# Loop loads moved behind the last weight turns, two more gradient buffers, and row halves in the head of a fused forward and backward block

## The chip, the cores and the metric

The kernel runs on one core of one Trainium2 chip. The time is the device time of one execution in microseconds (us); lower is better. A profile is one execution recorded instruction by instruction, and its span runs from the first to the last instruction.

## The reference

The reference returns the output of a block and all its gradients, for 2048 rows of width D = 576 and a hidden width F = 4608:

```python
mod = (_silu(c) @ w_mod).reshape(c.shape[0], 6, 1, -1)      # sa, ca, ga, sb, cb, gb
h = _layernorm(x) * (1 + ca) + sa
x = x + ga * irfft2(rfft2(h) * (w_r + 1j * w_i))
h = _layernorm(x) * (1 + cb) + sb
x = x + gb * einsum('bsf,fd->bsd', (h @ w_gate) * (h @ w_up), w_down)
...
_out, _vjp = jax.vjp(_f, A_x, A_w_r, A_w_i, B_w_gate, B_w_up, B_w_down, c, w_mod)
_grads = _vjp(grad_out)
```

What matters here is one product of the backward pass: the gradient of the hidden layer, `ghh = (grad_out * gb) @ w_down^T`, of shape 2048 x 4608. Everything in the loop over the hidden width needs it.

## The kernel before

Rows are kept 128 to a tile, 16 tiles; the hidden width is cut in 36 blocks of 128 columns. The kernel has a head, a loop over the 36 blocks, and a tail.

**The head** does three things. It runs the forward spectral layer in three stages: stage 1 (`s1_*`) norms and transforms the rows, stage 2 (`s2_*`) filters, stage 3 (`s3_*`) transforms back, norms again and makes `h2p` (the second normed input); every fourth step of stage 3 turns four tiles of it into `h2T` with a transposing DMA on SP's queue (four such turns in all). Into these stages, and after them, it deals the `u4` work, which computes `ghh` block by block and stores it in `ghhT_d` in DRAM. The chip is kept busy with `u4` matmuls where the spectral stages wait; about half of `u4` is left when stage 3 ends, and is run to its end alone.

**The u4 work.** `goT` holds `grad_out * gb` turned by TensorE (PE) in stage 1 (16 tiles, five 128-column pieces each; width 576 is four and a half pieces, so the fifth piece is half padding). For two blocks at a time, `w_down` is loaded into `wdn` (two buffers) and turned by a transposing DMA into `wdT` (five buffers); these DMAs are in the list `turns`, 18 of them. One block is four groups; a group is five matmuls of 128x512 into one PSUM bank, one per piece, and a copy by ScalarE (ACT) or VectorE (DVE), in turn, from the bank into `ghh_st`. After four groups GpSimd (POOL) issues the store of `ghh_st`, 512 KB, to `ghhT_d`. `ghh_st` has two buffers, so the copies of a block wait until the store of the block two before it has landed. `u4` has three PSUM banks; the spectral stages have the other five (`fps`).

**The loop.** For each block it needs `wgu` (columns of `w_gate` and `w_up`, loaded for two blocks at a time, gate on SP's queue, up on POOL's), `ghh` (from `ghhT_d`, on POOL's queue), and for each four blocks `wT`, ten transposing DMAs of `w_gate` and `w_up` on SP's queue. The matmuls of `h2T` with `wgu` come first (`gup`); in them the half piece of width 64 is already done with row halves: gate's 64 rows sit on partitions 0 to 63 and up's on 64 to 127, so that two matmuls use one half of TensorE's rows each ("corners", L606). The `u8` matmuls, which need `wT`, start with the second block.

**What sets the order.** Each engine runs its instructions in one fixed order, which a scheduler in the compiler makes from priorities, buffers and dependences. `tc.issue_after(i)` adds the condition that what follows stands behind `i` on `i`'s engine. In the kernel before, the loop's first loads have no such condition, and the first `wT` is tied to the seventh- to third-last turns: the loads of `wgu` and `ghh` for the first blocks come to stand in the queues in the middle of the `u4` work, between the last two `h2T` turns.

Of the kernel before, what the change touches and what calls it, by code (L numbers as in the profile page):

```python
# [19 lines left out]
NT = 16  # L20
S = 2048
D = 576
DP = 640
# [59 lines left out]
def build(ctx, tc, A_x, A_w_r, A_w_i, B_w_gate, B_w_up, B_w_down, c_in, w_mod, grad_out,  # L83
          out_0, out_1, out_2, out_3, out_4, out_5, out_6, out_7, out_8):
    nc = tc.nc
# [11 lines left out]
    def dram(name, shape, dt):  # L97
        return nc.dram_tensor(name, list(shape), dt).ap()
# [3 lines left out]
    modb_d = dram("modb_d", [128, 6, D], BF)  # L102
# [4 lines left out]
    ghhT_d = dram("ghhT_d", [F, S], BF)  # L107
# [4 lines left out]
    MSA, MCA, MGA, MSB, MCB, MGB = range(6)  # L112
# [8 lines left out]
    ident = glob.tile([128, 128], BF, name="ident")  # L121
# [12 lines left out]
    def evac(dst, src, eng=None):  # L134
        if eng is None:
            eng = "a" if cnt[0] % 2 == 0 else "v"
            cnt[0] += 1
        if eng == "a":
            nc.scalar.copy(dst, src)  # L139
        else:  # L140
            nc.vector.tensor_copy(dst, src)  # L141
# [42 lines left out]
    gonf = res2.tile([128, NT * D + 64], BF, name="gon")  # L184
    gon = gonf[:, 0:NT * D].rearrange("p (t d) -> p t d", t=NT)

    with ExitStack() as hs:
        def pool(name, bufs, side="left", space=None, stack=hs):
            kw = dict(name=name, bufs=bufs, reuse_waits="tile")
            if space is not None:  # L190
                kw["space"] = space
            else:
                kw["side"] = side
            return stack.enter_context(tc.tile_pool(**kw))

# [46 lines left out]
        def mod_make(j, wm, eng="v"):  # L242
            for h in range(2):
                ps = fps.tile([128, 512], FP32, name="modps", tag="fp")
                for m in range(5):
                    nc.tensor.matmul(ps[:, 0:288], lhsT=sc_rep[:, m, :], rhs=wm[:, m, h * 288:(h + 1) * 288], start=(m == 0), stop=(m == 4))
                if j in (MCA, MCB):
                    nc.vector.tensor_scalar(out=modh[j][:, h * 288:(h + 1) * 288], in0=ps[:, 0:288], scalar1=1.0, scalar2=None, op0=ADD)
                else:
                    evac(modh[j][:, h * 288:(h + 1) * 288], ps[:, 0:288], eng=eng)  # L250
            return nc.sync.dma_start(modb_d[:, j, :], modh[j][:]).ins
# [28 lines left out]
        Vv = VA[:].rearrange("k (g t c f) -> k g t c f", g=NG, t=NT, c=2)  # L280
        hTs, zts, n1s = {}, {}, {}
        gbT = hp1.tile([128, 5], BF, name="gbT")
        nc.gpsimd.memset(gbT[:], 0.0)

        def s1_norm(t):
            c4, tt = t // 4, t % 4
# [24 lines left out]
        def s1_cols(t):  # L311
            zt = zts[t] = hw2.tile([128, 2, FP], BF, name="zt", bufs=3)
            for cc in range(2):
                zp = fps.tile([128, 512], FP32, name="zp", tag="fp")
                for m in range(5):
                    mm = nc.tensor.matmul(zp[:, :FP], lhsT=hTs[t][:, m, :], rhs=T["RD"][:, m, cc, :], start=(m == 0), stop=(m == 4))  # L316
                evac(zt[:, cc, :], zp[:, :FP], eng="a")
            if t == 1:
                with tc.issue_after(mm.ins):
                    mod_make(MGB, wms[MGB], "a")  # L320
                with nc.allow_non_contiguous_dma(reason="tiny column load"):
                    nc.sync.dma_start(gbT[:, 0:4], modb_d[0, MGB, 0:512].rearrange("(m q) -> q m", q=128))
                    nc.sync.dma_start(gbT[0:64, 4:5], modb_d[0, MGB, 512:576].rearrange("(m q) -> q m", q=64))

        def s1_rows(t):
            zt = zts[t]
# [14 lines left out]
        nc.gpsimd.dma_start(wn_d, wn[:].rearrange("k c a f -> k (c a f)"))  # L341
        goT = u4.tile([128, NT, 5, 128], BF, name="goT")
        for t in range(NT):
            pt = u4ps.tile([128, 5, 128], BF, name="u4p")
            for m in range(5):
                nc.tensor.transpose(pt[:, m, :], gonf[:, t * D + m * 128:t * D + (m + 1) * 128], ident[:])
            nc.vector.tensor_tensor(out=goT[:, t, :, :], in0=pt[:], in1=gbT[:].unsqueeze(2).to_broadcast([128, 5, 128]), op=MUL)
        FB4 = 2
        turns, wdTs, sts, u4_done, u4r = [], {}, {}, [0], []

        def u4_group(g, eng=None):
            fb, sb4 = g // 4, g % 4
            k, j = fb // FB4, fb % FB4
            if g % (4 * FB4) == 0:
                wdTs[k] = (u4w if not u4r or k % 5 < 2 else u4r[0]).tile([128, FB4, 5, 128], BF, name="wdT")
                wdn = wdn2[:, k % 2, :, :]
                with tc.issue_after(first):
                    nc.sync.dma_start(wdn[:, :, 0:D], B_w_down[fb * 128:(fb + FB4) * 128, :].rearrange("(j f) d -> f j d", f=128))
                turns.append(nc.sync.dma_start_transpose(out=wdTs[k][:].rearrange("q j m f -> q (j m) f"), in_=wdn.rearrange("f j d -> f (j d)")).ins)
            if sb4 == 0:  # L360
                sts[fb] = u4w.tile([128, NT, 128], BF, name="ghh_st", bufs=2)
            pt = u4ps.tile([128, 4, 128], FP32, name="u4p")
            for m in range(5):
                nc.tensor.matmul(pt[:], lhsT=wdTs[k][:, j, m, :], rhs=goT[:, 4 * sb4:4 * sb4 + 4, m, :], start=(m == 0), stop=(m == 4))  # L364
            evac(sts[fb][:, 4 * sb4:4 * sb4 + 4, :], pt[:], eng=eng)
            if sb4 == 3:
                nc.gpsimd.dma_start(ghhT_d[fb * 128:(fb + 1) * 128, :], sts[fb][:].rearrange("f t p -> f (t p)"))

        def u4_groups(n, eng=None):
            for _ in range(n):  # L370
# [70 lines left out]
            T["IR"] = load_table(hp1, "IR", "tA")  # L441
        r2.close()
        u4r.append(pool("u4r", 3, "right"))
        hw2 = pool("hc3", 2, "right")


# [60 lines left out]
    with ExitStack() as ms:  # L507
# [13 lines left out]
        with ExitStack() as bs:  # L521
            FBW = 2
# [112 lines left out]
            def u8_output(fbs, t, h):  # L635
# [8 lines left out]
                else:  # L644
                    nc.vector.tensor_tensor(out=dst, in0=dst, in1=pu[:, 0:288], op=ADD)  # L645

            for fb in range(NFB):
                if fb % FBW == 0:
                    wgu = wp.tile([128, 9, FBW * 128], BF, name="wgu")
                    for wi_, wsrc in enumerate((B_w_gate, B_w_up)):  # L650
                        eng = nc.sync if wi_ == 0 else nc.gpsimd
                        eng.dma_start(wgu[:, 4 * wi_:4 * wi_ + 4, :], wsrc[0:512, fb * 128:(fb + FBW) * 128].rearrange("(m q) f -> q m f", q=128))
                        eng.dma_start(wgu[64 * wi_:64 * wi_ + 64, 8, :], wsrc[512:576, fb * 128:(fb + FBW) * 128])
                if fb == 0:
                    wTs[0] = wT_load(0, turns[-7:-2])
                ghh = ghp.tile([128, NT, 128], BF, name="ghh")
                nc.gpsimd.dma_start(ghh[:].rearrange("f t p -> f (t p)"), ghhT_d[fb * 128:(fb + 1) * 128, :])
                trip[fb] = [p.tile([128, NT, 128], BF, name=nm) for p, nm in ((tp2, "gT"), (tp2, "uT"), (tp, "hhT"), (tp, "ggT"), (tp, "guT"))] + [ghh, wgu]
                main = gup_items(fb, 0)
                if fb >= 2:  # L660
                    main += product(fb - 2, 2)
                main += gup_items(fb, 1)
                turn_at = len(main)
                main.append(turn_items(fb))
                if 1 <= fb < NFB - 1:
                    main += product(fb - 1, 0) + product(fb - 1, 1)
                outs = [(fb - 1, t, h) for t in range(NT) for h in range(2)] if 1 <= fb < NFB - 1 else []
                dealt = 0
                for k, f in enumerate(main):
# [17 lines left out]
    with ExitStack() as ts:  # L687
# [383 lines left out]
        for tp_ in range(NT // 2):  # L1071
# [13 lines left out]
            for ti in range(2):  # L1085
                t = 2 * tp_ + ti
# [16 lines left out]
                stored = nc.gpsimd.dma_start(o0_v[:, t, :], o0[:])  # L1103
# [87 lines left out]
```

## Time and profile before

| | |
|---|---|
| median of 3 runs | 1605.65 us (1599.14 to 1614.77) |
| the profiled execution | 1611.72 us, of which the span is 1609.9 us |
| mean granted TensorE clock | 0.989 |
| PE busy | 1542.1 us (96%) |
| stretch with least PE work in the head | 200 to 250 us: PE busy 33.59 of 50 us, clock 0.83 |
| first matmul of the loop | 298.05 us |

Busy time of PE is modelled from pipelined matmuls; a stretch in which PE shows less than its full length is one in which it had nothing to run. The granted clock is the share of full speed that the throttle allowed. A DMA's "time to landing" is from its issue to its last semaphore update.

### The profile page before, as it was taken

What the parts mean: (1) busy time and instruction counts of PE and PEld (TensorE: products, weight loads), DVE (VectorE), ACT (ScalarE), POOL (GpSimd) and SP (SyncE); (2) the same over time, 40 slices, a digit from 0 to 9 for tenths busy, and PEclk for the clock granted to TensorE, in tenths of its full rate; (3) what the DMA queues carried; (4) which work ended last, traced back from release to release, by engine and by line L of the source; (5) the groups of instructions that cost most, each with busy time, mean ns of one, the idle gap of its engine ahead of it and who ended that gap; (6) DMA issues with size and microseconds to landing.
All of it is one profiled execution on the core that took longest, in us unless ns stands there. A gap on an engine that the chain in (4) does not pass through costs nothing.

```text
span 1609.9 us, 29989 instructions
## 1 busy us (share of the span) xinstructions
PE 1542.1 (96%) x11354; PEld 1041.0 (65%) x11354; DVE 1038.4 (65%) x2610; ACT 559.1 (35%) x1108; POOL 170.4 (11%) x284
## 2 busy tenths in 40 slices
PE   6999959999999999999999999999999979899997
PEld 4666624466766666666766666666667666677775
DVE  6765743566666666666666666666666765678656
ACT  6666712322222222222222222222222365466022
POOL 0001311100101010000101010100100011100232
PEclk9999979999999999999999999999999999999998
DMA  9978998488778677685767877776866786636775
GB/s 320 278 213 230 266 191 193 134 149 158 146 149 145 139 145 151 129 165 116 159 149 136 159 138 146 137 164 114 169 123 132 193 256 195 227 114 180 281 216 162
DMA packets 482995, 280.36 MB, mean 174 GB/s; under 512 B 405377, under 2 KB 450178, under 8 KB 481954
## 3 DMA queue, kind: packets, MB, share of 16 engines
q1 hardware_dynamic: 457666, 185.38, 55.4%
q0 software_dynamic: 25184, 93.07, 19.6%
q8 instruction: 88, 1.44, 0.4%
q14 instruction: 57, 0.47, 0.1%
HBM read 108.51 MB, written 82.31 MB: 119 GB/s over the span
## 4 chain that ended last, share of the span: by engine, by line
PE 77%; DMA 11%; DVE 5%; ACT 3%; issue 3%; POOL 0%; SPq 0%; DVEq 0%; ACTq 0%; POOLq 0%
PE u57p L558 25%; PE u8p L640 17%; PE gup L611 15%; PE u4p L364 7%; DMA ghhT_d<-ghh_st 2%; PE gup L606 2%; PE u3p L1091 2%; DMA Xn<-xn_d 2%; DMA n2c<-n_d 1%; DMA wdB<-in_B_w_down_dram 1%; DMA xc<-in_A_x_dram 1%; DMA x1t<-x_d 1%; PE yp L471 1%; PE zp L316 1%; PE yp L1000 1%
## 5 line engine op out<-in xcount | busy, mean ns | idle before, releaser
L645 DVE TENSOR_TENSOR acc<-acc,u8p 128x288 f32<-128x288 f32 x1088 | 488.6, 453 | 315.1 <-PE u8p L640 314.7
L640 PE MATMUL u8p<-wT,ggT 128*128 128x288 bf16 x1152 | 327.5, 286 | 1.2 <-DVE acc L645 1.2
L640 PE MATMUL u8p<-wT,guT 128*128 128x288 bf16 x1152 | 327.2, 286 | 0.0
L611 PE MATMUL gup<-h2T,wgu 128*128 128x512 bf16 x1152 | 295.4, 379 | 0.0
L561 ACT CAST so<-u57p 128x288 bf16<-128x288 f32 x216 | 86.0, 398 | 520.6 <-PE u57p L558 512.3
L558 PE MATMUL u57p<-gon,hh_sf 128*128 128x288 bf16 x1152 | 188.6, 286 | 0.2 <-DMA hh_sf<-hhT 0.2
L558 PE MATMUL u57p<-h2p,gg_sf 128*128 128x288 bf16 x1152 | 187.6, 286 | 0.0
L558 PE MATMUL u57p<-h2p,gu_sf 128*128 128x288 bf16 x1152 | 186.3, 286 | 0.0
L364 PE MATMUL u4p<-goT,wdT 128*128 128x512 bf16 x720 | 165.2, 384 | 18.6 <-ACT ghh_st L139 15.6
L611 PEld LDWEIGHTS <-wgu 128*128 128x128 bf16 x1152 | 109.5, 98 | 98.9 <-issue 17.5
L640 PEld LDWEIGHTS <-ggT 128*128 128x128 bf16 x1152 | 112.6, 98 | 67.2 <-issue 14.0
L640 PEld LDWEIGHTS <-guT 128*128 128x128 bf16 x1152 | 112.7, 98 | 55.3 <-issue 1.8
L1091 PEld LDWEIGHTS <-hl 128*128 128x128 bf16 x1152 | 111.7, 98 | 36.5 <-issue 8.5
L364 PEld LDWEIGHTS <-wdT 128*128 128x128 bf16 x720 | 70.2, 99 | 98.1 <-issue 23.6
L558 PEld LDWEIGHTS <-hh_sf 128*128 128x128 bf16 x1152 | 112.6, 98 | 28.8 <-DMA hh_sf<-hhT 0.5
L558 PEld LDWEIGHTS <-gu_sf 128*128 128x128 bf16 x1152 | 112.5, 98 | 28.4
L558 PEld LDWEIGHTS <-gg_sf 128*128 128x128 bf16 x1152 | 112.5, 98 | 28.3
L613 ACT CAST gT<-gup 128x512 bf16<-128x512 f32 x144 | 84.4, 586 | 129.7 <-PE gup L611 129.7
L613 ACT CAST uT<-gup 128x512 bf16<-128x512 f32 x144 | 84.3, 585 | 75.9 <-PE gup L611 73.0
L1091 PE MATMUL u3p<-wdB,hl 128*128 128x288 bf16 x672 | 95.3, 289 | 6.5 <-DMA wdB<-in_B_w_down_dram 5.6
L141 DVE CAST ghh_st<-u4p 128x512 bf16<-128x512 f32 x56 | 38.7, 690 | 75.0 <-PE u4p L364 55.4
L624 POOL DMA_DIRECT2D hhT_d<-hhT x36 | 33.2, 921 | 505.2 <-DVE hhT L615 476.2
(356 smaller groups left out, 1726.7 us busy)
## 6 DMA issues: line engine op xcount, KB each, us to landing
ghhT_d<-ghh_st POOLq DMA_DIRECT2D x36, 512.0 KB, 4.7
ghh<-ghhT_d POOLq DMA_DIRECT2D x36, 512.0 KB, 7.6
hhT_d<-hhT POOLq DMA_DIRECT2D x36, 512.0 KB, 6.7
hl<-hhT_d SPq DMA_DIRECT2D x32, 576.0 KB, 7.4
out_dram<-woT SPq DMA_DIRECT2D x72, 128.0 KB, 2.0
wdn<-in_B_w_down_dram SPq DMA_DIRECT2D x18, 288.0 KB, 3.6
out_dram<-so SPq DMA_DIRECT2D x36, 144.0 KB, 2.6
wgu<-in_B_w_up_dram POOLq DMA_DIRECT2D x18, 256.0 KB, 5.6
```

What stands on the lines that cost most here:

```text
L141: nc.vector.tensor_copy(dst, src)
L316: mm = nc.tensor.matmul(zp[:, :FP], lhsT=hTs[t][:, m, :], rhs=T["RD"][:, m, cc, :], start=(m == 0), stop=(m == 4))
L364: nc.tensor.matmul(pt[:], lhsT=wdTs[k][:, j, m, :], rhs=goT[:, 4 * sb4:4 * sb4 + 4, m, :], start=(m == 0), stop=(m == 4))
L558: mm = nc.tensor.matmul(pw[0][:, 0:288], lhsT=sf[:, t, :], rhs=rhs_n[:, t, h * 288:(h + 1) * 288], start=(t == 0), stop=(t == NT - 1))
L561: nc.scalar.copy(so[:, h * 288:(h + 1) * 288], pw[0][:, 0:288])
L606: nc.tensor.matmul(pts[-1][:], lhsT=wgu[r, 8, jw * 128:(jw + 1) * 128], rhs=h2T[r, 4 * sb4:4 * sb4 + 4, 4, :], start=True, stop=False)
L611: nc.tensor.matmul(pts[k][:], lhsT=wgu[:, 4 * wi_ + m, jw * 128:(jw + 1) * 128], rhs=h2T[:, ts_, m, :], start=False, stop=(m == 3))
L613: nc.scalar.copy((gT, uT)[wi_][:, ts_, :], pts[k][:])
L624: nc.gpsimd.dma_start(hhT_d[:, :, fb, :].rearrange("tp f x -> f tp x"), hhT[:].rearrange("f (tp ti) p -> f tp (ti p)", ti=2))
L640: nc.tensor.matmul(pu[:, 0:288], lhsT=l_, rhs=r_, start=(k == 0), stop=(k == len(mms) - 1))
L645: nc.vector.tensor_tensor(out=dst, in0=dst, in1=pu[:, 0:288], op=ADD)
L1091: mm = nc.tensor.matmul(p2[:, 0:288], lhsT=hls[fb // 9][:, fb % 9, ti * 128:(ti + 1) * 128], rhs=(wdA[:, fb] if fb < 15 else wdB[:, fb - 1 ...
```

## The change

Four things are changed, all in the head.

First, `later(q, fb)` puts the loop's loads for blocks 0, 1 and 2 behind the u4 work: those on SP's queue behind the third-last of the 18 turns (for blocks 0 and 1) and behind the last (for blocks 2 and 3), those on POOL's queue behind the 26th, 29th and 32nd store of 36. The first `wT` comes behind the last turn.

Second, `ghh_st` has four buffers once stage 2 is over: blocks with `fb % 4 >= 2` take theirs from a new pool `u4s`.

Third, blocks 20 to 35 (`TWICE = 20`) do their half piece with row halves. The load of `w_down` writes its last 64 columns twice, so that after the turn they stand on partitions 0 to 63 and 64 to 127. A block then begins with four matmuls of 64 rows, one per group and bank, alternately on the two halves, and each group has four full matmuls where it had five. A block takes four banks at its start: `fps` banks for odd blocks, three `u4` banks and one `fps` bank for even ones.

Fourth, for this `goT` and `gbT` need the half piece on partitions 64 to 127 too: stage 1 has a sixth PE transpose per tile and a second, small DVE multiplication; `gbT` is filled by a third tiny load where a memset filled it with zeros.

```diff
-                    nc.sync.dma_start(gbT[0:64, 4:5], modb_d[0, MGB, 512:576]...)
+                    for r in (0, 64):
+                        nc.sync.dma_start(gbT[r:r + 64, 4:5], modb_d[0, MGB, 512:576]...)
...
-            pt = u4ps.tile([128, 5, 128], BF, name="u4p")
-            for m in range(5):
-                nc.tensor.transpose(pt[:, m, :], gonf[:, t * D + m * 128:t * D + (m + 1) * 128], ident[:])
-            nc.vector.tensor_tensor(out=goT[:, t, :, :], in0=pt[:], in1=gbT[:].unsqueeze(2).to_broadcast([128, 5, 128]), op=MUL)
+            pt = u4ps.tile([128, 6, 128], BF, name="u4p")
+            for m in range(6):
+                c0 = t * D + m * 128 if m < 5 else t * D + 448
+                nc.tensor.transpose(pt[:, m, :], gonf[:, c0:c0 + 128], ident[:])
+            nc.vector.tensor_tensor(out=goT[:, t, :, :], in0=pt[:, 0:5, :], in1=gbT[:].unsqueeze(2).to_broadcast([128, 5, 128]), op=MUL)
+            nc.vector.tensor_tensor(out=goT[64:128, t, 4, :], in0=pt[64:128, 5, :], in1=gbT[64:128, 4:5].to_broadcast([64, 128]), op=MUL)
...
+                    if fb >= TWICE:
+                        nc.sync.dma_start(wdn[:, :, D:DP], rows[:, :, 512:D])
...
-                sts[fb] = u4w.tile([128, NT, 128], BF, name="ghh_st", bufs=2)
-            pt = u4ps.tile([128, 4, 128], FP32, name="u4p")
-            for m in range(5):
-                nc.tensor.matmul(pt[:], lhsT=wdTs[k][:, j, m, :], rhs=goT[:, 4 * sb4:4 * sb4 + 4, m, :], start=(m == 0), stop=(m == 4))
+                sts[fb] = (u4w if not u4r or fb % 4 < 2 else u4r[1]).tile([128, NT, 128], BF, name="ghh_st", bufs=2)
+            if fb >= TWICE and sb4 == 0:
+                pts = [(fps if fb % 2 else u4ps).tile([128, 4, 128], FP32, name="u4p", tag="fp" if fb % 2 else "u4p") for _ in range(3)] + [fps.tile([128, 4, 128], FP32, name="u4p", tag="fp")]
+                for q in range(4):
+                    r = slice(64 * (q % 2), 64 * (q % 2) + 64)
+                    nc.tensor.matmul(pts[q][:], lhsT=wdTs[k][r, j, 4, :], rhs=goT[r, 4 * q:4 * q + 4, 4, :], start=True, stop=False)
+                u4r[2:] = pts
+            pt = u4r[2 + sb4] if fb >= TWICE else u4ps.tile([128, 4, 128], FP32, name="u4p")
+            n = 4 if fb >= TWICE else 5
+            for m in range(n):
+                nc.tensor.matmul(pt[:], lhsT=wdTs[k][:, j, m, :], rhs=goT[:, 4 * sb4:4 * sb4 + 4, m, :], start=(m == 0 and n == 5), stop=(m == n - 1))
...
+        u4r.append(pool("u4s", 2, "right"))
...
+            def later(q, fb):
+                es = ExitStack()
+                if fb < 3:
+                    es.enter_context(tc.issue_after((turns[-3 + fb], stored[25 + 3 * fb])[q]))
+                return es
...
-                    wTs[0] = wT_load(0, turns[-7:-2])
+                    wTs[0] = wT_load(0, turns[-1:] * 5)
```

The loads of `wgu` and `ghh` in the loop stand in `with later(...)`; they are otherwise the same.

More of the change, by code (lines that the diff above doesn't have):

```diff
@@ L282, in build @@
         gbT = hp1.tile([128, 5], BF, name="gbT")
-        nc.gpsimd.memset(gbT[:], 0.0)
         def s1_norm(t):
@@ L322, in s1_cols @@
                     nc.sync.dma_start(gbT[:, 0:4], modb_d[0, MGB, 0:512].rearrange("(m q) -> q m", q=128))
-                    nc.sync.dma_start(gbT[0:64, 4:5], modb_d[0, MGB, 512:576].rearrange("(m q) -> q m", q=64))
+                    for r in (0, 64):
+                        nc.sync.dma_start(gbT[r:r + 64, 4:5], modb_d[0, MGB, 512:576].rearrange("(m q) -> q m", q=64))
         def s1_rows(t):
@@ L343, in build @@
         for t in range(NT):
-            pt = u4ps.tile([128, 5, 128], BF, name="u4p")
-            for m in range(5):
-                nc.tensor.transpose(pt[:, m, :], gonf[:, t * D + m * 128:t * D + (m + 1) * 128], ident[:])
-            nc.vector.tensor_tensor(out=goT[:, t, :, :], in0=pt[:], in1=gbT[:].unsqueeze(2).to_broadcast([128, 5, 128]), op=MUL)
+            pt = u4ps.tile([128, 6, 128], BF, name="u4p")
[4 more added lines that the diff above has]
+            nc.vector.tensor_tensor(out=goT[64:128, t, 4, :], in0=pt[64:128, 5, :], in1=gbT[64:128, 4:5].to_broadcast([64, 128]), op=MUL)
         FB4 = 2
-        turns, wdTs, sts, u4_done, u4r = [], {}, {}, [0], []
+        TWICE = 20
+        turns, stored, wdTs, sts, u4_done, u4r = [], [], {}, {}, [0], []
         def u4_group(g, eng=None):
@@ L357, in u4_group @@
                 with tc.issue_after(first):
-                    nc.sync.dma_start(wdn[:, :, 0:D], B_w_down[fb * 128:(fb + FB4) * 128, :].rearrange("(j f) d -> f j d", f=128))
+                    rows = B_w_down[fb * 128:(fb + FB4) * 128, :].rearrange("(j f) d -> f j d", f=128)
+                    nc.sync.dma_start(wdn[:, :, 0:D], rows)
+                    if fb >= TWICE:
+                        nc.sync.dma_start(wdn[:, :, D:DP], rows[:, :, 512:D])
                 turns.append(nc.sync.dma_start_transpose(out=wdTs[k][:].rearrange("q j m f -> q (j m) f"), in_=wdn.rearrange("f j d -> f (j d)")).ins)
             if sb4 == 0:
-                sts[fb] = u4w.tile([128, NT, 128], BF, name="ghh_st", bufs=2)
-            pt = u4ps.tile([128, 4, 128], FP32, name="u4p")
-            for m in range(5):
-                nc.tensor.matmul(pt[:], lhsT=wdTs[k][:, j, m, :], rhs=goT[:, 4 * sb4:4 * sb4 + 4, m, :], start=(m == 0), stop=(m == 4))
+                sts[fb] = (u4w if not u4r or fb % 4 < 2 else u4r[1]).tile([128, NT, 128], BF, name="ghh_st", bufs=2)
[9 more added lines that the diff above has]
+                nc.tensor.matmul(pt[:], lhsT=wdTs[k][:, j, m, :], rhs=goT[:, 4 * sb4:4 * sb4 + 4, m, :], start=(m == 0 and n == 5), stop=(m == n - 1))
             evac(sts[fb][:, 4 * sb4:4 * sb4 + 4, :], pt[:], eng=eng)
             if sb4 == 3:
-                nc.gpsimd.dma_start(ghhT_d[fb * 128:(fb + 1) * 128, :], sts[fb][:].rearrange("f t p -> f (t p)"))
+                stored.append(nc.gpsimd.dma_start(ghhT_d[fb * 128:(fb + 1) * 128, :], sts[fb][:].rearrange("f t p -> f (t p)")).ins)
         def u4_groups(n, eng=None):
@@ L651, in build @@
                         eng = nc.sync if wi_ == 0 else nc.gpsimd
-                        eng.dma_start(wgu[:, 4 * wi_:4 * wi_ + 4, :], wsrc[0:512, fb * 128:(fb + FBW) * 128].rearrange("(m q) f -> q m f", q=128))
-                        eng.dma_start(wgu[64 * wi_:64 * wi_ + 64, 8, :], wsrc[512:576, fb * 128:(fb + FBW) * 128])
+                        with later(wi_, fb):
+                            eng.dma_start(wgu[:, 4 * wi_:4 * wi_ + 4, :], wsrc[0:512, fb * 128:(fb + FBW) * 128].rearrange("(m q) f -> q m f", q=128))
+                            eng.dma_start(wgu[64 * wi_:64 * wi_ + 64, 8, :], wsrc[512:576, fb * 128:(fb + FBW) * 128])
                 if fb == 0:
-                    wTs[0] = wT_load(0, turns[-7:-2])
+                    wTs[0] = wT_load(0, turns[-1:] * 5)
                 ghh = ghp.tile([128, NT, 128], BF, name="ghh")
-                nc.gpsimd.dma_start(ghh[:].rearrange("f t p -> f (t p)"), ghhT_d[fb * 128:(fb + 1) * 128, :])
+                with later(1, fb):
+                    nc.gpsimd.dma_start(ghh[:].rearrange("f t p -> f (t p)"), ghhT_d[fb * 128:(fb + 1) * 128, :])
                 trip[fb] = [p.tile([128, NT, 128], BF, name=nm) for p, nm in ((tp2, "gT"), (tp2, "uT"), (tp, "hhT"), (tp, "ggT"), (tp, "guT"))] + [ghh, wgu]
```

## The prediction

> **What bounds the kernel now.** I read the page first: PE is busy nearly throughout, so only a stretch in which PE has nothing to run, or PE work taken away, can move the time.
>
> ```profile
> PE 1542.1 (96%) x11354; PEld 1041.0 (65%) x11354; DVE 1038.4 (65%) x2610; ACT 559.1 (35%) x1108; POOL 170.4 (11%) x284
> ```
>
> Then the stages by windows. The head is full (49 to 50 of 50 us) from 50 us on except at 200 to 250 us. In pieces of 5 us (columns: stretch, its length, busy time of PE, weight loads, DVE, ACT, POOL, granted clock, DMA share, GB/s):
>
> ```profile
> 205.00:210.00 5.00, 2.42 (x7) 0.70 (x6) 3.84 (x12) 2.14 (x4) 1.85 (x3) 0.77 1.20 117
> 215.00:220.00 5.00, 0.08 (x1) 0.00 (x0) 0.00 (x0) 0.00 (x0) 0.00 (x0) 0.79 1.18 176
> 220.00:225.00 5.00, 0.00 (x0) 0.00 (x0) 0.00 (x0) 0.00 (x0) 1.42 (x3) 0.50 1.35 72
> 225.00:230.00 5.00, 1.11 (x3) 0.40 (x3) 1.75 (x5) 1.07 (x2) 0.00 (x0) 0.50 1.30 83
> ```
>
> All engines stand still, the DMA engines are full and move little (72 to 83 GB/s; 282 at 70 to 80 us), and the clock falls to 0.50. The timeline of PE from there to the loop:
>
> ```profile
> 204.69 0.59 PE L364 MATMUL u4p<-goT,wdT 128*128 128x512 bf16 x2
> 207.86 7.22 PE L364 MATMUL u4p<-goT,wdT 128*128 128x512 bf16 x25 [2.58 <-DVE ghh_st L141]
> 228.89 31.68 PE L364 MATMUL u4p<-goT,wdT 128*128 128x512 bf16 x140 [13.81 <-ACT ghh_st L139]
> 262.35 35.77 PE L364 MATMUL u4p<-goT,wdT 128*128 128x512 bf16 x165 [1.77 <-ACT ghh_st L139]
> 298.05 0.60 PE L606 MATMUL gup<-h2T,wgu 64*128 64x512 bf16 x3
> ```
>
> PE waits for copies out of PSUM, and the waits of 195 to 300 us say what those wait for:
>
> ```profile
> ACT ghh_st L139 <- DMA ghhT_d<-ghh_st: 33.4, 6, 17.5
> DVE ghh_st L141 <- DMA ghhT_d<-ghh_st: 17.5, 2, 13.8
> ```
>
> The bound of this stretch is thus the store of a finished block: with two buffers the copies of a block need the store of two blocks before. The chain of waits confirms it: the store issued at 208.33 landed 19.82 us later and ends the 13.81 us wait. Median landing is 4.7 us.
>
> What slowed it stands in POOL's and SP's queues just ahead: at 198.70 to 200.54 us POOL issues the loop's up weights (288 KB) and two blocks of ghh (512 KB each), and at 198.87 SP issues the third h2T turn. That turn lands after 30.8 us; the first, second and fourth, among the same stores but without these loads, take 9.8, 12.1 and 7.2 us.
>
> **The stall.** From 204.69 to 298.05 us are 93.36 us and 332 matmuls. The last run of 165 takes 35.77 us, 0.216 us each; 332 at that rate are 71.7 us. So 21.7 us are lost: 2.58 + 13.81 + 1.77 = 18.2 idle, the other 3.5 at a reduced clock. Two parts of the change act on it independently. (a) The loads leave: in the changed order seven ghhT_d stores follow the last n2 store on POOL's queue before a load comes, and on SP's the gate weights stand behind the turn of blocks 30 and 31. The third h2T turn then has the company of the second: I take 12.1 us, and stores of 7.4 (the median at 180 to 198 us). (b) Four buffers: a block takes 20 matmuls, 4.3 us, so a store may now take some three blocks, 13 us, plus about a block of PSUM room, instead of 4.3 plus room. Either alone covers most of it; I remove 21.7. The bounds are 16 (below, first rival) and 21.7.
>
> **Row halves.** The loop's corners are the same form, and the timeline shows a set of four between full matmuls:
>
> ```profile
> 307.29 0.81 PE L611 MATMUL gup<-h2T,wgu 128*128 128x512 bf16 x3
> 308.03 0.61 PE L606 MATMUL gup<-h2T,wgu 64*128 64x512 bf16 x4
> 308.57 0.82 PE L611 MATMUL gup<-h2T,wgu 128*128 128x512 bf16 x3
> ```
>
> The third full matmul starts at 307.29 + 2 x 0.216 = 307.72, the next after the corners at 308.57: 0.85 us where one step is 0.216, so four corners cost 0.63 us. Four full ones cost 0.86. Gain 0.23 per block, 16 blocks: 3.7 us. (The Trainium skill, TensorEngine Tiling (Array Packing), Theoretical Speedup, promises up to 2x for a contraction of at most 64; that would be two of four steps, 0.43 a block and 6.9 us. The same page under Key Properties says that a change of tiling mode drains TensorE; the 0.31 us into and out of the corners agree with that, and I go by the row.) Against it: block 20 begins while its banks are still being copied; its corners are not all paired and wait for a copy of 0.69 us, and at the loop's start one corner waits for the last block's copy. Estimated 0.5 each from that row, together 1.0.
>
> **Stage 1.** 16 PE transposes: a run of 14 of the same (L346) takes 0.94 us, 0.07 each, so 1.1 us, on a PE that is 95% busy. 16 DVE products 64x128 from PSUM: not in the trace; the nearest row is a DVE copy 128x128 from PSUM, 214 ns; the 128x640 product takes 814. That is 3.4 us of DVE by the near row (13 by the far one, taken as an unlikely end). DVE is full from 40 to 47 us, but between 55 and 63 us idles 0.9 to 1.3 us of each 2.5 us waiting for PE; about half is hidden. The last goT products run to 66.3 us, and PE's first u4 matmul at 64.94 waits 0.26 us for one. I charge 2.0; bounds 0 and 6.
>
> **The rest.** Eight extra loads of 128-byte rows (32 KB) on SP: 0.4 us of issue, and they land before a turn. Not in the trace; bounds nothing and 3.6 us each (the whole 288 KB load beside them). They lie in a chain with room: with the loop starting at 298.05 - 22.4 = 276 (the sum below), PE needs the turn for blocks 28 and 29 eight blocks of 4.1 us earlier, at 243, and by the rows (h2T issue 6.4, wdT landing 8 to 11, load 4) it lands at about 236; the later ones have 7 us or more. I charge nothing; cover gone, each us late is a us of PE.
>
> The ten wT turns now stand last on SP's queue. In before they took from 241.00 to 263.87 with turns between; now, behind that chain, I put them at 251 to 270. The first u8 matmul comes 11 us after the loop's start (309.23 against 298.05), so they are due at about 287: hidden, 17 us to spare. The moved wgu and ghh loads of the first two blocks go out between 230 and 250 and are due at 276 and later. From the loop's first matmuls on, every engine's order is the one of before, so no other term.
>
> Sum: -21.7 - 3.7 + 1.0 + 2.0 = -22.4. On the profiled execution, 1611.72, that is 1589.3. This execution is 6.1 above the median of 1605.65. If its excess is a worse stall, the median run has 16 to win; if not, 22. One profile can't tell; I go between, -19.5 on the median: **1586**.
>
> **Rivals.**
>
> *The turn stays slow whatever its company.* For it: at 220 to 230 us, with the loads landed, the DMA still moves 72 to 83 GB/s. Against: three other h2T turns beside stores took 7 to 12 us. Price: the store of 208.33 lands at 228.2; with four buffers PE gets to about 223 before it needs that buffer, a stall of 5 us plus 1 of clock. Gain 16 instead of 22: 1595.7 on the profiled basis, 1590 to 1592 on the median.
>
> *The wait moves to the w_down turns.* Without the store's wait PE runs 20 us ahead of where it was, while h2T and wdT turns alternate on one queue with two wdn buffers. For it: wdT at 214.74 took some 17 us. If two steps of the chain take 17 in place of 11, the 7 us of room turn to a stall of 5 to 10: 1594 to 1599 on the profiled basis, 1590 to 1597 on the median.
>
> *Slower: the wT turns come too late.* They stand behind everything else on SP. Should they land after 287, PE waits at the first u8 matmul, and the gain is spent when they land at 309: from there on slower. That needs the ten turns to take 58 us instead of the 23 of before, or the last w_down turn to go out 40 us later. Price when it bites: 40 us late is 18 slower, 1624 on the median. Against: even the slow stretch delayed SP by no more than 20.
>
> *It doesn't do what it says.* The row halves bring nothing if the pairs don't overlap (four corners at 0.216 plus drains: +0.42 a block, 6.7 us lost instead of 3.7 won): gain 12, 1593 to 1599.
>
> **Chances.** Forecast 0.55 (own range 1577 to 1592), slow turn 0.15, late w_down turns 0.14, no overlap 0.06, late wT 0.06, the rest unexplained 0.04. The range for 8 in 10 is 1575 to 1601; its lower end is the full 22 with noise of the runs (1599 to 1615 before), the upper takes in the rivals but the slower one. Within 1% is what a measurement of this kernel can't tell from no change; 1% here is 1589.6. The forecast is mostly below, the first two rivals on the line: faster 0.58, same 0.34, slower 0.08.
>
> **What would show it.** Right: between 200 us and the loop PE has no gap over 1 us and a clock of 1.00; the loop's first L620 matmul starts near 276; the third h2T turn lands in 9 to 14 us; the waits of ACT and DVE for ghhT_d are gone; a set of corners takes 0.6 us; goT's small products take 0.2 us each. Wrong: PE waits for wdT or wT, a first u4 matmul later than 67 us, or the stall in the same place.

## The result and the profile after

The changed kernel takes 1592.36 us (median of 11 runs, 1588.48 to 1600.53), the kernel before 1609.51 us in the 11 runs taken with it. The ratio on record is 0.9912 (95% interval 0.9886 to 0.9938): 0.6 to 1.1% less, inside or at the edge of the 1% that the prediction called measurable. It is not quite the ratio of the two medians, which are 17 us apart; 0.9912 is 14 us. Below, a gain "by the ratio" is the one on record. The profiled execution took 1594.8 us with a span of 1593.0, 16.9 less than the profiled span of before. Forecast were 1586 and, on the profiled basis, 1589.3: the gain came, but 5 to 6 us smaller (2 us by the medians).

The page of the changed kernel, its line of engines:

```profile
PE 1535.0 (96%) x11370; PEld 1035.0 (65%) x11370; DVE 1045.6 (66%) x2626; ACT 559.8 (35%) x1108; POOL 170.3 (11%) x283
```

PE is 7 us less busy (1542.1 before), about what the row halves (3.5) and the matmuls that ran at a reduced clock (3.5) come to. DVE is 7 us busier, with 16 instructions more. The same stretches of 5 us (stretch, length, busy time of PE, weight loads, DVE, ACT, POOL, granted clock, DMA share, GB/s):

```profile
205.00:210.00 5.00, 5.00 (x28) 2.59 (x27) 1.07 (x4) 1.62 (x4) 0.54 (x1) 1.00 1.14 248
210.00:215.00 5.00, 1.52 (x7) 0.48 (x5) 3.84 (x12) 1.96 (x4) 1.08 (x2) 1.00 0.95 226
215.00:220.00 5.00, 4.56 (x20) 1.59 (x20) 4.96 (x15) 1.50 (x3) 1.40 (x3) 1.00 0.99 291
220.00:225.00 5.00, 5.00 (x26) 1.99 (x24) 5.00 (x12) 1.65 (x3) 0.54 (x1) 1.00 1.11 259
225.00:230.00 5.00, 5.00 (x27) 1.80 (x26) 1.92 (x4) 1.28 (x3) 0.53 (x1) 1.00 1.04 258
```

PE is nearly full where it stood still, the clock is 1.00, and in the four pieces that the prediction shows the DMA engines, about as full as before, move 248 to 291 GB/s in place of 72 to 176. But from 210 to 215 us, where it had been full (4.98 us), PE now runs for 1.52 us. The timeline of PE from the end of stage 3 to the loop:

```profile
205.80 4.48 PE L377 MATMUL u4p<-goT,wdT 128*128 128x512 bf16 x20
213.04 1.24 PE L377 MATMUL u4p<-goT,wdT 128*128 128x512 bf16 x5 [2.76 <-DVE ghh_st L141]
215.35 1.24 PE L377 MATMUL u4p<-goT,wdT 128*128 128x512 bf16 x5 [1.07 <-DVE ghh_st L141]
...
221.18 0.60 PE L372 MATMUL u4p<-goT,wdT 64*128 64x512 bf16 x4
221.72 3.63 PE L377 MATMUL u4p<-goT,wdT 128*128 128x512 bf16 x16
225.28 0.61 PE L372 MATMUL u4p<-goT,wdT 64*128 64x512 bf16 x4
...
282.64 0.39 PE L620 MATMUL gup<-h2T,wgu 64*128 64x512 bf16 x1
```

The loop starts at 282.64 instead of 298.05 us, 15.4 earlier. The waits of 13.81 and 1.77 us are gone. A block in row halves runs from 221.18 to 225.28, 4.10 us, where a full one takes 20 x 0.216 = 4.32. But the gap that was 2.58 us is still there, now 2.76 and 1.07, and stage 3 ends later: its last yp matmul ends at 205.96 us instead of 200.97. From there to the loop 20.4 us are saved; ahead of it 5.0 are lost, of which the prediction had 2.0. Both losses are seen on DVE:

```profile
208.96 0.46 DVE L501 TENSOR_TENSOR x<-x,xc 128x576 bf16<-128x576 bf16 x1 [3.89 <-DMA xc<-in_A_x_dram]
...
212.34 0.64 DVE L141 CAST ghh_st<-u4p 128x512 bf16<-128x512 f32 x1
```

From 205.06 to 208.96 us DVE runs nothing: the next instruction in its order is a product of stage 3 that needs `xc`, the rows of `x` that stage 3 loads again. The copy out of PSUM for which PE waits at 210.28 stands behind that product and the norm after it. The small products of stage 1 (duration ns min/median/max, first and last start), and what waited for them (us in total, times):

```profile
L349 DVE TENSOR_TENSOR goT<-u4p,gbT x16: 289/295/295, 42.5 to 69.7; 64x128 bf16<-64x128 bf16 x16
...
  PEld L347: 1.6, 2
  PE u4p L347: 1.6, 3
  PEld L377: 1.0, 1
  PE u4p L377: 0.5, 1
```

They take 0.295 us each, 4.7 in all, and PE waits for them: the first u4 matmul comes at 68.08 us instead of 64.94.

### The profile page after: what moved, and what is told of

The parts are those of the page before. It is cut to its first block, busy times and chain, and to the rows that moved or that the text cites. A ratio compares the mean times of both kernels' runs of the same rounds, so it can differ in the third digit from the quotient of the medians.

```text
span 1593.0 us, 30039 instructions
## 1 busy us (share of the span) xinstructions
PE 1535.0 (96%) x11370; PEld 1035.0 (65%) x11370; DVE 1045.6 (66%) x2626; ACT 559.8 (35%) x1108; POOL 170.3 (11%) x283
## 4 chain that ended last, share of the span: by engine, by line
PE 77%; DMA 9%; DVE 7%; issue 3%; ACT 2%; SPq 0%; POOL 0%; DVEq 0%; ACTq 0%; POOLq 0%
PE u57p L572 26%; PE u8p L654 17%; PE gup L625 16%; PE u4p L377 7%; PE gup L620 2%; DMA xc<-in_A_x_dram 2%; DMA n2c<-n_d 2%; DMA Xn<-xn_d 2%; DMA wmj<-in_w_mod_dram 1%; DMA wdB<-in_B_w_down_dram 1%; DVE pr L803 1%; PE u3p L1113 1%; PE yp L485 1%; PE yp L1022 1%; PE zp L315 1%
## 5 line engine op out<-in xcount | busy, mean ns | idle before, releaser
L377 PE MATMUL u4p<-goT,wdT 128*128 128x512 bf16 x656 | 151.1, 379 | 4.4 <-DVE ghh_st L141 3.8
L377 PEld LDWEIGHTS <-wdT 128*128 128x128 bf16 x656 | 61.9, 98 | 77.2 <-issue 11.5
L139 ACT CAST ghh_st<-u4p 128x512 bf16<-128x512 f32 x88 | 51.1, 585 | 68.1 <-PE u4p L377 67.7
```

## The experiments

The theory after the result had these parts: the loads beside the third h2T turn made the stall, and moving them or adding buffers each removes most of it; the row halves gain 3.5 us and stage 1 gives that back; DVE's order at `xc` keeps the rest. The rivals: the turn is slow whatever its company, and the new gaps are the draw of one execution. "Loop" below is the start of the loop's first matmul in the profiled execution, "rest" the span from there to the end, "third h2T" the time of that turn from issue to landing, "stall" the sum of PE's gaps over 0.15 us between the last yp matmul and the loop.

```
                                 third h2T  stall  loop    rest     ratio to before (95%)
before                            30.8      18.2   298.05  1311.9
before, profiled again            13.6      10.3   289.96  1317.4
loads moved alone                 13.4       5.7   286.53  1310.6   0.9951 (0.9926-0.9976)
buffers alone                     22.6       7.7   289.37  1314.8   0.9944 (0.9917-0.9972)
row halves alone                  17.7       7.5   286.09  1313.6   0.9945 (0.9920-0.9970)
loads and buffers                 13.4       0     278.50  1309.9   0.9925 (0.9902-0.9949)
  the same order again             7.6       0     279.01  1312.6   0.9937 (0.9911-0.9963)
whole change                       8.6       3.8   282.64  1310.4   0.9912 (0.9886-0.9938)
  again                           10.4       0     276.22  1322.0   0.9918 (0.9885-0.9951)
whole, cheaper stage 1            10.3       0     274.91  1314.2   0.9920 (0.9886-0.9954)
  the same order again            11.2       0     280.22  1307.9   0.9912 (0.9882-0.9943)
whole, cheaper stage 1, xc POOL    7.8       0     272.78  1313.3   0.9910 (0.9875-0.9945)
```

**Loads moved alone.** The edits of the change around the loop's loads and the wT turns, nothing else:

```
-                    wTs[0] = wT_load(0, turns[-7:-2])
+                    wTs[0] = wT_load(0, turns[-1:] * 5)
...
+                with later(1, fb):
+                    nc.gpsimd.dma_start(ghh[:]..., ghhT_d[fb * 128:(fb + 1) * 128, :])
```

> Only the first loads of the loop and the wT turns are moved behind the w_down turns; two buffers and full matmuls stay. Theory (the loads' company made the third h2T turn and the stores slow): the third h2T turn lands in 8 to 13 us instead of 30.8, the gaps 13.81 and 1.77 us and the fall of the clock go, a gap of about 2.6 us near 205 us stays; 15 to 19 us less than before. Rival (the turn is slow whatever its company, and the four buffers alone hid it): the third turn takes 25 us or more, PE still waits some 14 us for a store, 0 to 4 us less.

1595.18 us against 1605.43: 10 us less by the medians, 8 by the ratio, where 15 to 19 were expected. The third turn lands in 13.4 us, and the long gap goes, but not all waits for stores do. The timeline of PE:

```profile
209.33 4.48 PE L364 MATMUL u4p<-goT,wdT 128*128 128x512 bf16 x20 [0.74 <-DVE ghh_st L141]
216.78 31.95 PE L364 MATMUL u4p<-goT,wdT 128*128 128x512 bf16 x140 [2.97 <-ACT ghh_st L139]
...
255.14 31.46 PE L364 MATMUL u4p<-goT,wdT 128*128 128x512 bf16 x145 [1.76 <-ACT ghh_st L139]
```

Against the profiled execution of before the loop comes 11.5 us earlier: with two buffers a store of 9 to 10 us, without any load of the loop beside it, already stops PE for 3.

**Buffers alone.**

```
-                sts[fb] = u4w.tile([128, NT, 128], BF, name="ghh_st", bufs=2)
+                sts[fb] = (u4w if not u4r or fb % 4 < 2 else u4r[1]).tile([128, NT, 128], BF, name="ghh_st", bufs=2)
...
+        u4r.append(pool("u4s", 2, "right"))
```

> Only the four buffers for finished blocks; the loads stay where they were. Theory: the third h2T turn still takes 25 to 31 us and the clock still falls; PE runs two blocks (8.6 us) further before it needs the slow store, so 13.81 + 1.77 us of waits shrink to 5 to 7: 9 to 13 us less. Rival (the buffers carry the gain by themselves): no wait for a store at all, 15 to 19 us less. Second rival (PE waits for the w_down turns in the same slow stretch instead): 0 to 6 us less, PE's gap put down to wdT.

1595.61 us, 9 us less by the ratio, the lower end of the theory's 9 to 13. The loads did not all stay where they were: with the new buffers the order on two queues came out otherwise, so that POOL issues the up weights of blocks 0 and 1 at 212 to 220 us instead of 199, and SP the first gate weights at 241 instead of 221. So when the third turn goes out, only the two loads of ghh stand beside it. The turn takes 22.6 us all the same, the two stores behind it 20.2 and 17.8, and PE stops once for a store:

```profile
209.23 1.24 PE L364 MATMUL u4p<-goT,wdT 128*128 128x512 bf16 x5 [0.67 <-DVE ghh_st L141]
211.54 13.11 PE L364 MATMUL u4p<-goT,wdT 128*128 128x512 bf16 x60 [1.07 <-DVE ghh_st L141]
230.61 58.84 PE L364 MATMUL u4p<-goT,wdT 128*128 128x512 bf16 x265 [5.95 <-ACT ghh_st L139]
```

PE runs 60 matmuls into the slow stretch and then waits 5.95 us, about the 5 us that the prediction worked out for a turn that stays slow. So the buffers hide much of a slow stretch and do not cure it. This execution, 1605.97 us, was the slowest of its twelve.

**Row halves alone.** L361 to L377 and the lines of stage 1 as in the change, loads and buffers as before.

> Only the row halves of the last 16 blocks and what stage 1 needs for them (a sixth transpose and a small product for each tile, 128-byte loads); loads and buffers as before. Theory: blocks in row halves take 4.1 us instead of 4.32, 3.5 us less; stage 1 gives 2.5 to 3.1 us of it back (first u4 matmul near 68 instead of 65 us); the stall stays: 1 us less to 1 us more. Rival (the delay of stage 1 is swallowed by the stall, which ends with a transfer): 2 to 4 us less. Rival (stage 3 pays as well): 1 to 4 us more.

1596.78 us, 9 us less by the ratio and clear of noise, which neither the theory nor its rivals gave. In the profile the third turn took 17.7 us, and PE waited 4.35 us where before waited 13.81:

```profile
225.48 1.07 PE L372 MATMUL u4p<-goT,wdT 64*128 64x512 bf16 x3 [4.35 <-ACT ghh_st L139]
```

That the stall of one execution was another can't explain medians of 12 and 33 runs. The trace shows something that the theory had left out. ACT's waits for stores from 195 to 300 us (total, times, longest), here and in the second profile of before that is shown next:

```profile
ACT ghh_st L139 <- DMA ghhT_d<-ghh_st: 35.1, 9, 13.4
```

```profile
ACT ghh_st L139 <- DMA ghhT_d<-ghh_st: 20.2, 5, 10.3
```

Of the longest wait PE lost 4.35 of 13.4 us here, 13.81 of 17.5 and 6.80 of 10.3 in the two profiles of before. So PE ran on for 9.0 us into that wait, in place of 3.7 and 3.5. In row halves a block takes its banks from both pools, three and five, where `u4` had only three: the row halves are also room between PE and the copies, as the buffers are. How much of the 9 us is that room stays open, since no run has the banks without the row halves.

**The kernel before, profiled again.** No edit; its expectation was written after the results so far.

> The kernel before as it is, profiled once more. The prediction took 21.7 us of stall from one execution that was 6 us above the median. If the stall varies from run to run, this one shows another length of the third h2T turn (12 to 30 us) and a stall of 5 to 20 us, with the same 1311 to 1313 us from the loop's first matmul to the end; if the stall is fixed, 18 us of gaps again.

The stall varies. The same program, its timeline of PE:

```profile
206.81 4.48 PE L364 MATMUL u4p<-goT,wdT 128*128 128x512 bf16 x20 [1.29 <-DVE ghh_st L141]
218.09 10.66 PE L364 MATMUL u4p<-goT,wdT 128*128 128x512 bf16 x40 [6.80 <-ACT ghh_st L139]
230.99 59.04 PE L364 MATMUL u4p<-goT,wdT 128*128 128x512 bf16 x265 [2.25 <-ACT ghh_st L139]
```

The stall is 10.3 us, not 18.2, and the loop starts 8.1 us earlier. Yet this execution took 1610.12 us against 1611.72: what it won in the head it lost behind the loop's start, where 1317.4 us were left and not 1311.9, outside the 1311 to 1313 expected. The waits of PE from 300 us on (total, times, longest), before, first execution:

```profile
PE csA L747 <- DMA n2c<-n_d: 7.5, 4, 5.1
PE gcp L1127 <- DVE gcd L1123: 6.7, 1, 6.7
PE u3p L1091 <- DMA wdB<-in_B_w_down_dram: 5.6, 2, 4.3
```

and second:

```profile
PE u3p L1091 <- DMA wdB<-in_B_w_down_dram: 9.5, 1, 9.5
PE csA L747 <- DMA n2c<-n_d: 7.9, 5, 4.7
PE gcp L1127 <- DVE gcd L1123: 6.7, 1, 6.7
```

The wait for DVE (gcd) is the same to a tenth, the wait for a load (wdB) is 4 us longer. So two executions differ by several us in places where they wait for transfers, and one profile can't tell which of its stalls is typical.

**Loads and buffers, without row halves.** The edits of the first two experiments together.

> Loads moved and four buffers, no row halves and nothing added to stage 1. Theory (row halves 3.4 less, stage 1 2.5 to 3.1 more): within 1 us of the whole change, 14 to 18 us less than before, and hardly apart from the loads alone, since no store is late any more. First u4 matmul back near 65 us, third h2T turn 8 to 13 us. If stage 1 also made the gaps of stage 3 (1.1 us before, 3.5 after the whole change), they are 1 to 2 us here and the kernel is up to 3 us faster than the whole change.

1591.46 us, 0.9925 (0.9902 to 0.9949). Between the last yp and the loop PE has no gap over 0.15 us at all, and the loop starts at 278.50, between the two profiles of the whole change (282.64 and 276.22). Against the loads alone it is 4 us less, where "hardly apart" was expected. In the medians it can't be told apart from the whole change. So these two parts carry most of the gain, 12 of 14 us by the ratios; what the row halves add beside them, less what they cost in stage 1, is too small for this comparison. The gaps of stage 3 are 3.4 us here, against 3.5 in the whole change and 1.1 before: that they come from stage 1 isn't borne out.

**Cheaper stage 1.** The second copy of the last 64 columns at partitions 64 to 127 is made by transposing columns 448 to 575 first and then columns 512 to 575 over the lower half of the same bank, so one product for each tile is enough:

```
-            for m in range(6):
-                c0 = t * D + m * 128 if m < 5 else t * D + 448
-                nc.tensor.transpose(pt[:, m, :], gonf[:, c0:c0 + 128], ident[:])
...
+            nc.tensor.transpose(pt[:, 4, :], gonf[:, t * D + 448:t * D + 576], ident[:])
+            nc.tensor.transpose(pt[0:64, 4, :], gonf[:, t * D + 512:t * D + 576], ident[:])
+            nc.vector.tensor_tensor(out=goT[:, t, :, :], in0=pt[:], in1=gbT[:].unsqueeze(2).to_broadcast([128, 5, 128]), op=MUL)
```

> The whole change with a cheaper stage 1: the upper copy of the last 64 columns is written by the order of two PE transposes into one bank, so each tile keeps one product on DVE and the 16 small products are gone; six transposes remain. Theory (the small products of 0.295 us cost stage 1 and, by the shift, stage 3 their time): first u4 matmul 65.0 to 66.2 us instead of 68.1, loop's first matmul 2 to 4 us earlier than in the whole change, 1588 to 1590 us. Rival (the transposes are the cost, or stage 3 swallows the gain): first u4 matmul after 67 us or less than 1 us gained.

1591.93 us, 0.9920 (0.9886 to 0.9954): in the median the same as the whole change, where 1588 to 1590 us were expected. The first u4 matmul came at 66.91 us, between the theory's 65.0 to 66.2 and the rival's 67. All the profiles together size it. The last trv transpose, the end of stage 2, up to which nothing else differs, comes at 123.9 to 125.5 us (mean of six 124.6) with stage 1 as before, at 127.5 to 127.7 (three, 127.6) with the change's, and at 125.8 to 126.5 (three, 126.2) with the cheaper one. So stage 1 costs 3.0 us, of which this version takes away 1.4; the 1.6 that stay go with the transposes. A gain of that size is not to be seen in the medians.

**An earlier load of xc.** The two lines that make and load `xc` were written two steps of stage 3 earlier, on top of the cheaper stage 1:

```
+            if sa % 2:
+                xc = xcs[sa // 2] = hw2.tile([128, 2, D], BF, name="xc")
+                nc.sync.dma_start(xc[:], x_v[:, sa - 1:sa + 1, :])
...
```

> The kernel of the cheaper stage 1, and the loads of xc issued two steps of stage 3 (some 8 us) earlier. Theory (DVE stands in order at the product that waits for xc, and the copies behind it keep PE): no wait of DVE for xc over 0.5 us, PE's idle time from 140 to 220 us falls from 7.3 us in the whole change to 2 to 3.5, 3 to 5 us less than with the cheaper stage 1 alone. Rival (DVE is late anyway and the wait only moves, to the w_down turn now behind xc on SP): within 1 us, PE's gaps put down to wdT or still to ghh_st.

1593.26 us, 0.9912 (0.9882 to 0.9943), and nothing learnt of the theory: the edit did not reach the program, for every engine's order is the one of the kernel without it. The run is a second draw of the cheaper stage 1, and shows how far draws differ: DVE waited 11.2 us in sum for `xc`, 5.58 at most, where the first draw had 3.7, and the loop started at 280.22 instead of 274.91.

**The same without row halves.**

> Loads moved and four buffers without row halves, and xc issued two steps earlier. Theory: DVE's waits for xc (7.5 us in sum) go, PE's idle time of 140 to 220 us falls from 3.4 us to under 2: 1 to 2 us less than without the earlier xc. Against the kernel with row halves, cheaper stage 1 and earlier xc: 16 transposes of 0.07 less (1.1), row halves 3.4 more: 2 to 3 us slower than that. Rival (row halves bring nothing in the end): the two are within 1 us.

1596.31 us, 0.9937 (0.9911 to 0.9963). Here too every order is the one of the loads and buffers alone, so it repeats that run: loop at 279.01 (278.50), rest 1312.6 (1309.9). It was run beside the kernel with the row halves, the cheaper stage 1 and the same edit, and was 3.1 us slower (1593.26), where the theory had 2 to 3 and the rival, that row halves bring nothing, under 1. The intervals of the two overlap, so this leans to the theory and doesn't settle it.

**xc on POOL's queue.** This does move it: POOL's order has the load behind the store of `x1` of the pair before, and no w_down turn stands ahead of it.

```
-            nc.sync.dma_start(xc[:], x_v[:, s0:s0 + 2, :])
+            nc.gpsimd.dma_start(xc[:], x_v[:, s0:s0 + 2, :])
```

> The whole change with the cheaper stage 1, and the loads of xc on POOL's queue instead of SP's. Theory (on SP the load of xc stands behind a wdn load that waits for a w_down turn; DVE then stands in order at x<-x,xc, and the copies out of PSUM queue behind it): DVE's waits for xc between 140 and 220 us (13.0 us in sum in the whole change, 3.7 and 11.2 in two executions with the cheaper stage 1) fall under 2, PE idles under 2.5 us from 140 to 220 us, and the loop's first matmul comes at 273 to 276 us; 2 to 5 us less than the whole change. Rival (xc's own landing of 4 to 9 us is what DVE waits for, or POOL's stores hold it as long): the sum of waits stays at 4 to 13 us and nothing is gained.

In the trace the theory holds to the letter: DVE waits nowhere for `xc` from 140 to 220 us, PE has no gap over 0.15 us from 66.2 us to the loop, and the loop starts at 272.78 us, the earliest of all. The row of DVE's timeline that had waited 3.89 us:

```profile
201.01 0.46 DVE L501 TENSOR_TENSOR x<-x,xc 128x576 bf16<-128x576 bf16 x1
```

The median is 1590.89 us, 0.9910 (0.9875 to 0.9945); the whole change, run beside it, has 1590.42. The 2 to 5 us are not to be seen in the medians. With intervals of 4 to 6 us to either side and 14 us between the least and the most "rest" in the table, a gain of that size in the head isn't shown by these runs, and isn't excluded.

**The whole change again.**

> The whole change as it is, once more, beside the run above. If the gaps of stage 3 and at 210 to 215 us are the draw of one execution, the waits of DVE for xc have another sum than 13.0 us and the loop's first matmul lies between 277 and 284 us; the delay of stage 1 (first u4 matmul 4.6 us after the first trv against 0.6 in the kernel before) is there again, since it is DVE's work and not a transfer's. Ratio to the kernel before again 0.988 to 0.994.

1590.42 us, 0.9918 (0.9885 to 0.9951). The delay of stage 1 is there again (first u4 matmul 4.61 us after the first trv), and the gaps of 210 to 215 us are not: DVE waits 5.8 us in sum for `xc` instead of 13.0. The loop starts at 276.22, a shade earlier than expected. This execution, 1600.01 us, was the slowest of its ten. Most of that is a slow stretch that now sits elsewhere. The ten wT turns (from issue to landing, us):

```profile
DMA to landing us min/median/max: 12.3/17.8/21.1
```

In the first profile of the same kernel:

```profile
DMA to landing us min/median/max: 4.8/6.2/8.1
```

The stores of 245 to 280 us took 12.4 to 16.8 us instead of 2.9 to 7.2, and the wait that four buffers had removed came back at the loop's start (timeline of ACT, then of PE):

```profile
278.90 0.59 ACT L627 CAST gT<-gup 128x512 bf16<-128x512 f32 x1 [2.85 <-DMA wT<-in_B_w_up_dram]
286.30 0.59 ACT L627 CAST uT<-gup 128x512 bf16<-128x512 f32 x1 [6.81 <-DMA ghhT_d<-ghh_st]
```

```profile
286.94 1.07 PE L620 MATMUL gup<-h2T,wgu 64*128 64x512 bf16 x3 [5.81 <-ACT uT L627]
```

The first copy into `uT` waits for the store of a last block; the likely reason, which the profile doesn't show, is that `uT` takes the room of its buffer. Behind the wait 16 matmuls take 6.08 us, where the first profile has 3.63, at a clock of 0.61 to 0.71: 8.3 us lost in all. The last wT turn landed at 290.1 us, 5.0 ahead of the first u8 matmul at 295.14.

## Why the prediction was right, and where it was wrong

**The number.** 1592.36 lies just above the 1577 to 1592 that the text gave its own forecast, and beside the 1590 to 1592 that it gave the slow turn. The traces show that it was not a slow turn, so the number alone would have named the wrong cause. By the text's own line of 1%, 0.9912 falls on the side of "same" (0.34) and not of "faster" (0.58).

**The place and the two cures: right.** Without the loads the third h2T turn takes 7.6 to 13.4 us in eight profiles, with them, or the two of ghh, 13.6 to 30.8 in four. The loads moved alone are 8 us faster and the buffers alone 9, "most of" the 10 to 12 of both, and with both no profile of seven has a wait of PE for a store ahead of the loop. The stalls of 5.7 and 7.7 us in the profiles of the parts are one draw each. The rival of a turn that stays slow whatever its company fell. But the pair that differs by the loads alone all but touches (13.4 against 13.6 and 30.8). And company is not the whole cause: in the whole change run again, the fourth h2T turn took 13.9 us and a w_down turn 13.3 at 211 to 230 us, before any load of the loop had gone out, and the loads' new place, among the wT turns, had its own slow stretch. What starts such a stretch was not found.

**"I remove 21.7": the term that was too large.** The step that failed is "I remove 21.7", and with it "I go between, -19.5 on the median". The 21.7 was one draw. The same count on the second profile of before gives 14.4: from 202.77 us to the loop at 289.96 are 87.2 us, and the 337 matmuls there, at 0.216, are 72.8. The page gave the hint (the execution was 6.1 us above its median) and the text took it up, but gave 16 as the lower end, from the slow-turn rival alone; 14.4 lies below that. With 14.4 and the other terms as measured (3.5, 0.6 and 3.0 below) the sum is -14.4 - 3.5 + 0.6 + 3.0 = -14.3, and 0.9912 is 14 us. That the two are so near is partly luck: 14.4 is a draw as 21.7 was, and the terms don't simply add, since loads, buffers and row halves, at 8 to 9 us each when alone, cover the same waits.

**"2.58 ... idle", put down to the store: wrong.** This gap outlived the change as 2.76 and 1.07 us. PE waited for a copy on DVE, and DVE's copy waited for no store; it stood in order behind a product that waited for `xc`, 4.09 us in before and 3.89 after. (At the same place in the second profile of before, the 1.29 us are a store's: DVE's copy waits 1.12 us for one.) The load of `xc` stands on SP behind a wdn load that waits for a w_down turn to land (after the change it was issued at 202.69 us, the wdn load at 201.59, and the turn of 189.03 landed at 201.57). With `xc` on another queue these waits were gone; on SP's queue they were 3.7 to 13.0 us in sum from 140 to 220 us in all eleven profiles. "No gap over 1 us" between 200 us and the loop failed with it, by the 2.76 and the 1.07.

**Row halves: the matmuls right, a side effect missed.** A block takes 4.10 us, 0.22 less than 4.32 (predicted 0.23); 3.5 us over 16 blocks. Its set of four half matmuls costs 4.10 - 16 x 0.216 = 0.64. The rival without overlap fell. The Trainium skill, TensorEngine Tiling (Array Packing), Key Properties, says that a change of tiling mode drains TensorE; the trace agrees as far as it goes, since four half matmuls take as long as three full ones (0.65) and not as two. The unpaired corners of block 20 and the handover to the loop were put at 1.0. They cost 0.6: where PE has no gap from the end of the last yp matmul to the loop, that stretch takes 75.67 us in both profiles without row halves and 72.73 or 72.74 in all four with them, 2.9 us less and not 3.5. What the prediction left out is the room of the extra banks (9.0 us of a wait covered in place of 3.5 to 3.7, in the one profile of row halves alone), by which they work on the stall too.

**"I charge 2.0" for stage 1: too small.** It cost 3.0, inside the bounds of 0 to 6. The products take 295 ns, not the 214 of the nearest row, 4.7 us in all; at the end of stage 1 each stands between PE and its next transpose or its first u4 matmul, and PE waits four times, 2.1 us in sum. Yet without them only 1.4 us came back, so more than "about half" was hidden. The 1.6 that stayed go with the transposes, which were put at 1.1 us of PE. The first u4 matmul at 68.08 is past the 67 that the text named as a sign of error. With 2.9 won by the row halves and 3.0 lost here, that part of the change brings nothing where nothing stalls. The ratios of the whole change and of loads and buffers (0.9912 and 0.9918 against 0.9925 and 0.9937) lean to a gain of 1 to 4 us, within their intervals.

**Late w_down turns: fell.** No profile has a wait of PE for wdT ahead of the loop. **Late wT turns: cost nothing, with less room than thought.** "Hidden, 17 us to spare" was 30 us in one execution (landed by 262.3, first u8 matmul at 292.75) and 5.0 in the other.

**What was not in the sum.** The gaps of stage 3 rose from 1.1 to 3.5 us in the first profile, but that is a draw too: 3.5 and 1.1 in the whole change, 1.3 and 6.0 with the cheaper stage 1, none with `xc` on POOL's queue. And from the loop's start to the end the profiles take 1307.9 to 1322.0 us, a spread as large as the whole gain; 8.3 of it is the wait for stores in the whole change run again.

## What to carry to other kernels

Where a stall waits for a transfer, its length in one profile is a draw: look for the same transfer under other company, profile the same program twice, and give the stall a range that holds both. When PE waits for a copy, ask first what stands ahead of that copy on its own engine. A change that is made to save matmuls can also change how many banks lie between PE and the copies; count them before and after. And small products added to an engine that the next stage waits for show at the stage's end, however idle the engine is on average.

## What was not expected of the hardware

The DMA engines, with busy shares of 0.99 to 1.35, moved 291 GB/s at one time and 72 at another, least where the share was highest: the 640 KB turn of h2T took 5.6 to 30.8 us, a 512 KB store 2.9 to 20.2.

A DVE product from PSUM of 64x128 takes 295 ns, and one of 128x640 takes 815 (814 to 825 in the medians of the profiles). As an estimate, on a straight line through the two, an element of a row costs 1.02 ns and each instruction 165 ns besides. The Trainium skill, Perfetto Trace Analysis, Optimizing Scalar/DVE Operations, gives a data-access overhead of some 125 ns for each instruction of DVE on PSUM, and says that the profiled latency is about twice this; the 165 ns lie between the two.
